# Sixteen partitions of the second K tile go through ScalarE's queue

## The chip, the cores and the metric

The kernel runs on one core of a Trainium2 chip. Five engines work side by side: TensorE (PE in the profile; its weight loads are PEld), VectorE (DVE), ScalarE (ACT), GpSimd (POOL) and SyncE (SP). Sixteen DMA engines move data between HBM and on-chip memory; transfers are issued from SyncE's queue (q1 in the profile) and from ScalarE's (q10). The metric is device time in microseconds, lower is better. The kernel before takes 335.68 us, the median of three runs (335.58 to 337.4).

## What is computed

Attention with grouped heads: 16 batches, 32 query heads over 8 K/V heads, 16 queries per head, 2048 keys, head size 128, all in bf16.

```python
B, Hq, Hkv, Sq, Sk, D = 16, 32, 8, 16, 2048, 128

def reference(q, k, v):
    rep = Hq // Hkv
    k = jnp.repeat(k, rep, axis=1)
    v = jnp.repeat(v, rep, axis=1)
    scores = jnp.einsum("bhqd,bhkd->bhqk", q, k) * D ** -0.5
    p = softmax(scores, axis=-1)
    return jnp.einsum("bhqk,bhkd->bhqd", p, v)
```

K and V are 64 MiB each; everything else is small beside them.

## The kernel before

The 128 pairs of batch and K/V head are taken two at a time, in 64 steps p = 0 to 63 (NP = 64). A step has one K tile and one V tile of 1 MiB, 128 partitions of 8 KB each. Queries come in 16 chunks of four steps, 128 KB each.

For a step, VectorE transposes the K tile (line 474, `KT<-Kn`), PE forms the scores (line 345), VectorE scales them and takes the minimum of the negated scores (line 494), GpSimd joins the two halves (lines 216 to 231), ScalarE takes the exponential (line 542), PE transposes the result (line 363), ScalarE copies that out of PSUM (line 553), and PE multiplies by V (line 415, line 404 in the last steps). The product runs four steps behind the scores (PVLAG = 4). ScalarE then normalises (line 566) and stores (line 573).

K tiles have eight buffers (`Kn`, NK = 8) and V tiles four (`Vb`, NV = 4). SyncE issues nearly all loads in one order written out by hand: the first query chunk (line 166), then for each t the K tile of step t, a query chunk when one is due three steps later, and the V tile of step t - 6 (VLAG = 6). K tile p is issued once the transpose of step p - 8 is done; V tile p once the product of step p - 4 is done; a wait stops everything behind it in SyncE's queue. The first two K tiles are loaded by a plain transfer of 128 rows (line 276), all later ones by the helper `load` (line 171).

Each K buffer has a semaphore, `sem_k`. A transfer adds 16 to the semaphore that it names when all of it has landed. VectorE's transpose of step p waits on it (line 473). After two query chunks are spread out (line 161, by VectorE and GpSimd), PE transposes them (line 378) and ScalarE evicts them (line 528).

ScalarE begins with a table load and a dummy exponential, then issues the second query chunk (in a loop of one round, lines 517 and 518), adds 16 to each of the eight store semaphores, and waits for PE's first query transposes.

Of the kernel before, what the change touches and what calls it, by code (L numbers as in the profile page):

```python
# [11 lines left out]
NK = 8  # L12
# [13 lines left out]
def bass_standalone__gqa_softmax__sampling_kernel(  # L26
# [34 lines left out]
    Kn = [sb(f"Kn{i}", [128, 32 * 128], BF16) for i in range(NK)]  # L61
# [23 lines left out]
    sem_k = [sem(f"sem_k{i}") for i in range(NK)]  # L85
# [26 lines left out]
    kf = k.rearrange("b h s d -> (b h s d)").rearrange("(r x) -> r x", x=4096)  # L112
# [8 lines left out]
    def steps(eng, step, end):  # L121
        for p in range(LO):
            step(p, p)
        with eng.Fori(LO, HI, LOOP) as base:
            for i in range(LOOP):
                step(base + i, LO + i)
        for p in range(HI, end):
            step(p, p)


    def v_tile(p):
        return Kn[p % 4 + (NP - 8) % NK] if p >= NP - 4 else Vb[p % NV]
# [26 lines left out]
    def spread(eng, c, b):  # L159
        src = Qn[c % NQ][:, :, 64 * b:64 * b + 64]  # L160
        return eng.tensor_copy(Q4[:, :, b, :, :], src.unsqueeze(2).to_broadcast([128, 4, 4, 64]))  # L161


    def load_q(eng, c, s):
        src = qf[bass.ds(512 * c, 512), :].rearrange("(a j) d -> a (j d)", j=4)
        eng.dma_start(Qn[s][:, :, :].rearrange("a j d -> a (j d)"), src).then_inc(sem_q[s], 16)  # L166


    def load(eng, dst, src, x, n):
        ap = lambda t, dims: eng.lower_ap_dma(bass.AP(t.tensor, t.offset, dims))  # L170
        return eng.add_instruction(mybir.InstDMACopy(  # L171
            name=nc.get_next_instruction_name(), engine=eng.engine, mode="Copy", queue="qSPDynamicHW",
            ins=ap(src, [[n * x, 128 // n], [1, 1], [1, n * x]]), outs=ap(dst, [dst.ap[0], [1, 1], [1, x]])))
# [3 lines left out]
    with nc.Block() as block:  # L177
# [90 lines left out]
        @block.sync  # L268
        def _(sp):
            def load_k(p):  # L270
                s = p % NK
                if p >= NK:
                    sp.wait_ge(sem_kt, p - NK + 1)
                src = kf[128 * p:128 * (p + 1), :]
                if p < 2:
                    ins = sp.dma_start(Kn[s][:, :], src)  # L276
                else:
                    ins = load(sp, Kn[s][:, :], src, 4096, 2)
                ins.then_inc(sem_k[s], 16)

            def load_v(p):
                if p >= NP - 4:
                    sp.wait_ge(sem_kt, p - 3)
                elif p >= NV:
                    sp.wait_ge(sem_pv, p - NV + 1)
                dst = v_tile(p)[:, :]
                done = sem_vx[p - NP + 4] if NP - 4 <= p < NP - 1 else sem_v[p % NV]
                if p < P4:
                    load(sp, dst, vf[128 * p:128 * (p + 1), :], 4096, 2).then_inc(done, 16)
                    return  # L290
                dst = dst.rearrange("a (g x) -> a g x", g=2)
                src = vf4[:, 2 * p:2 * p + 2, :]
                if p < NP - 1:
                    for h in range(2):
                        load(sp, dst[:, h, :], src[:, h, :], 2048, 2).then_inc(done, 16)
                    return
                for n, x in enumerate((slice(0, 1536), slice(1536, 2048))):
                    sp.dma_start(dst[:, :, x], src[:, :, x]).then_inc(sem_vl[n], 16)

            def store_held(p, n):  # L300
                sp.wait_ge(sem_nm, p + n + 1)
                dst = of[128 * p:128 * (p + n), :].rearrange("(x r) d -> r x d", x=n)
                sp.dma_start(dst, Oh[:, p - PH:p - PH + n, :]).then_inc(sem_oh, 16)

            load_q(sp, 0, 0)
            for t in range(NP + VLAG):
                if t < NP:
                    load_k(t)
                for c in range(2, NQC):
                    if t == 4 * c - QLEAD:  # L310
                        if c == NQ:
                            sp.wait_ge(sem_q4d, 2)
                        sp.wait_ge(sem_q4, max(2, 4 * c - 6))
                        load(sp, Qn[c % NQ][:, :, :], qf[512 * c:512 * (c + 1), :], 512, 2).then_inc(sem_q[c % NQ], 16)
                if 0 <= t - VLAG < NP:
                    load_v(t - VLAG)
            p = PH
            for n in HELD:
                store_held(p, n)
                p += n  # L320
            sp.wait_ge(sem_oh, 16 * len(HELD))
            for s in range(NO):
                sp.wait_ge(sem_o[s], 16 * (PH // NO + 1 + (s == NO - 1)))
# [140 lines left out]
        @block.vector  # L464
        def _(dve):
            def kt(p, i):
                src = Kn[i % NK][:, :].bitcast(F32)
                dst = KT[i % NKT][:, :]
                if isinstance(p, int) and p >= P4:

                    src = src.rearrange("p (m x y) -> p m x y", m=2, x=8)
                    dst = dst.rearrange("p (x m y) -> p m x y", m=2, x=8)
                dve.wait_ge(sem_k[i % NK], 2 * (p - i) + 16 * (i // NK + 1))
                ins = dve.transpose(dst, src)  # L474
                ins.then_inc(sem_kt, 1)

            def recip(p, i, n):
                s = i % NR
                dve.wait_ge(sem_sum[1], p + n)
                dve.reciprocal(rrec[:, s:s + n], rowsum[:, s:s + n]).then_inc(sem_rec, n)  # L480

            def step(p, i):
                known = isinstance(p, int)
                dve.wait_ge(sem_s, p + 1)
                if i >= 2:
                    dve.wait_ge(sem_exp, p - 1)
                for h in range(2):
                    if not known or p < P4:
                        dst = Sneg[i % 2][:, :].rearrange("p (t h g l e) -> p h g t l e", t=8, h=2, g=2, e=2)[:, h]
                        src = S_ps[:, 1024 * h:1024 * (h + 1)].rearrange("p (g t e l) -> p g t l e", g=2, t=8, e=2)  # L490
                    else:
                        dst = Sneg[i % 2][:, :].rearrange("p (h t g l f) -> p h g t l f", h=2, t=4, g=2, f=4)[:, h]
                        src = S_ps[:, 1024 * h:1024 * (h + 1)].rearrange("p (g t f l) -> p g t l f", g=2, t=4, f=4)
                    ins = dve.tensor_scalar(  # L494
                        dst, src,
                        -scale, None, op0=ALU.mult, op1=ALU.min, accum_out=own[:, i % NR, h:h + 1],
                    )
                ins.then_inc(sem_max, 1)
                if i >= 3 and i % 2:
                    recip(p - 3, i - 3, 2)  # L500
                if not known or p + 2 < NP:
                    kt(p + 2, i + 2)

            dve.wait_ge(sem_q[0], 16)
            spread(dve, 0, 1).then_inc(sem_q4d, 2)
            for p in range(2):
                kt(p, p)
            steps(dve, step, NP)
            for p in range(NP - 2, NP):
                recip(p, p, 1)  # L510

        @block.scalar
        def _(act):
# [2 lines left out]

            with act.Fori(1, 2, 1) as c:
                load_q(act, c, 1)

            for s in range(NO):  # L520
                act.nop(nofuse=True).then_inc(sem_o[s], 16)
# [106 lines left out]
```

## Time and profile before

| | before |
|---|---|
| median of three runs | 335.68 us (335.58 to 337.4) |
| the profiled execution: time | 335.8 us |
| the profiled execution: span from first to last instruction | 333.9 us |
| bytes moved, mean rate | 138.61 MB, 415 GB/s |
| busy share PE, VectorE, ScalarE, GpSimd | 84%, 88%, 78%, 45% |
| K loads: count, median from issue to landing | 64, 20.2 us |
| V loads of 1 MiB: the same | 56, 18.3 us |
| chain that ended last: DMA, PE, VectorE | 57%, 17%, 16% |

The span is cut into 40 slices of 8.3 us on the page. The chain that ended last is followed back from the last instruction: at each step to what released it. Its DMA part counts from a transfer's issue to its landing, so time that the transfer waited behind others is in it. A row of the timeline gives the start, the duration, the engine, the line, the operation, output and input, and in brackets how long the engine was idle before and what ended that. A row of the windows gives, for one stretch of the span, the busy time and count of PE, PEld, VectorE, ScalarE and GpSimd, then the granted PE clock, the mean busy share of the DMA engines (it can exceed 1 in a short window, because a packet is booked whole where it begins) and GB/s.

### The profile page before, as it was taken

The numbers are of one execution on the slowest core, as the hardware profiler recorded it, in microseconds if no ns is written. First come the engines' busy times: TensorE is split into PE (matmuls) and PEld (weight loads), VectorE is DVE, ScalarE is ACT, GpSimd is POOL, SyncE is SP. The second block draws the span as 40 slices with busy tenths as digits, with TensorE's granted clock in tenths as the row PEclk, the third lists the DMA queues.
The fourth block names the chain that finished last, engine by engine and source line by source line (L and its number), as shares of the span: only waits on it lengthen the run. The fifth ranks groups of instructions, "written<-read, shape, count | busy, mean of one in ns | idle before, by whom it ended". The sixth has DMA issues, their size and how long they took to land.

```text
span 333.9 us, 16112 instructions
## 1 busy us (share of the span) xinstructions
PE 279.1 (84%) x6542; PEld 209.1 (63%) x6542; DVE 294.8 (88%) x354; ACT 258.8 (78%) x482; POOL 149.4 (45%) x488
## 2 busy tenths in 40 slices
PE   2557979999998989888897988979879798788786
PEld 1234757777776766666665766757657567667464
DVE  3999998999999989989898898998999989999930
ACT  3286887989897979779688787887878787886873
POOL 4444455353645544354445435354363453543330
PEclk9996999999999999999999999999999999999999
DMA  8999999999999999999999999999999999999997
GB/s 316 422 412 432 413 412 426 418 425 422 426 422 431 427 422 425 423 422 425 420 426 421 424 422 426 430 417 428 421 425 422 426 420 418 426 422 413 409 408 261
DMA packets 21854, 138.61 MB, mean 415 GB/s; under 512 B 11472, under 2 KB 11984, under 8 KB 13136
## 3 DMA queue, kind: packets, MB, share of 16 engines
q1 hardware_dynamic: 14640, 136.69, 97.7%
q10 hardware_dynamic: 7200, 1.74, 2.4%
q8 instruction: 8, 0.13, 0.2%
q14 instruction: 6, 0.05, 0.0%
HBM read 136.31 MB, written 2.10 MB: 415 GB/s over the span
## 4 chain that ended last, share of the span: by engine, by line
DMA 57%; PE 17%; DVE 16%; issue 7%; ACT 1%; SPq 1%; POOL 1%; DVEq 0%; POOLq 0%
DMA Vb<-in_v_dram 44%; PE O_ps L415 10%; DVE KT L474 9%; DMA Kn<-in_k_dram 8%; DVE Sneg L494 7%; DMA Kn<-in_v_dram 5%; PE ST_ps L363 3%; PE S_ps L345 3%; ACT P L542 1%; SPq L171 1%; PE ST_ps L378 1%; PE ST_ps L404 0%; POOL nbias L224 0%; SPq L276 0%; SPq L166 0%
## 5 line engine op out<-in xcount | busy, mean ns | idle before, releaser
L474 DVE STREAM_TRANSPOSE KT<-Kn 128x2048 f32<-128x2048 f32 x64 | 147.7, 2308 | 21.0 <-DMA Kn<-in_k_dram 20.9
L542 ACT ACTIVATE P<-Sneg,nbias 128x1024 bf16<-128x1024 f32 x128 | 146.0, 1142 | 15.1 <-POOL nbias L224 13.2
L494 DVE TENSOR_SCALAR_CACHE_REDUCE Sneg<-S_ps 128x1024 f32<-128x1024 f32 x128 | 149.9, 1206 | 3.0 <-PE S_ps L345 2.8
L415 PE MATMUL O_ps<-Vb,PT 64*64 64x128 bf16 x3584 | 111.1, 216 | 30.9 <-issue 26.8
L415 PEld LDWEIGHTS O_ps<-Vb,PT 64*64 64x64 bf16 x3584 | 102.9, 107 | 49.9 <-issue 49.9
L553 ACT ACTIVATE PT<-ST_ps 128x512 f32<-128x512 f32 x126 | 68.5, 594 | 15.7 <-PE ST_ps L363 15.0
L345 PE MATMUL S_ps<-KT,Qs 32*64 32x512 bf16 x2048 | 74.3, 399 | 6.0 <-DVE Sneg L494 3.9
L363 PE MATMUL ST_ps<-ident,P 128*128 128x128 f32 x504 | 69.7, 282 | 8.3 <-ACT P L542 8.3
L216 POOL COPY oth<-own 64x4 f32<-64x4 f32 (+1 forms) x65 | 11.9, 183 | 136.4 <-DVE Sneg L494 134.3
L363 PEld LDWEIGHTS ST_ps<-ident,P 128*128 128x128 f32 x504 | 54.7, 142 | 16.6 <-ACT P L542 10.9
L345 PEld LDWEIGHTS S_ps<-KT,Qs 32*64 32x64 bf16 x2048 | 27.6, 106 | 30.5 <-issue 17.1
L198 POOL COPY Qs<-QT 128x512 bf16<-128x512 bf16 x64 | 39.0, 610 | 12.1 <-POOL rowsum L231 6.0
L224 POOL TENSOR_SCALAR nbias<-own,oth 128x1 f32<-128x1 f32 x128 | 33.9, 280 | 10.6 <-POOL oth L219 9.0
L566 ACT ACTIVATE O<-O_ps,rrec 128x128 bf16<-128x128 f32 x48 | 17.5, 365 | 26.6 <-PE O_ps L415 26.5
L161 POOL COPY Q<-Qn 128x1024 bf16<-128x1024 bf16 x31 | 32.4, 1044 | 1.3 <-DMA Qn<-in_q_dram 1.3
L231 POOL TENSOR_TENSOR rowsum<-own,oth 64x1 f32<-64x1 f32 x128 | 23.8, 186 | 8.2
L378 PEld LDWEIGHTS ST_ps<-ident,Q 128*128 128x128 f32 x128 | 14.4, 148 | 18.3 <-issue 18.3
L378 PE MATMUL ST_ps<-ident,Q 128*128 128x128 f32 x128 | 22.1, 300 | 4.5 <-POOL Q L161 4.5
L542 ACT ACTIVATION_READ_ACCUMULATOR P<-Sneg,nbias 128x1 f32 x128 | 24.1, 188 | 0.0
L528 ACT ACTIVATE QT<-ST_ps 128x512 f32<-128x512 f32 x32 | 18.5, 578 | 3.7 <-PE ST_ps L378 3.7
L219 POOL COPY oth<-own 64x4 f32<-64x4 f32 (+1 forms) x65 | 11.8, 181 | 7.3
L566 ACT ACTIVATE Oh<-O_ps,rrec 128x128 bf16<-128x128 f32 x12 | 4.4, 367 | 9.6 <-PE O_ps L415 6.7
(30 smaller groups left out, 44.6 us busy)
## 6 DMA issues: line engine op xcount, KB each, us to landing
Kn<-in_k_dram SPq DMA_DIRECT2D x64, 1024.0 KB, 20.2
Vb<-in_v_dram SPq DMA_DIRECT2D x56, 1024.0 KB, 18.3
Vb<-in_v_dram SPq DMA_DIRECT2D x8, 512.0 KB, 15.6
Kn<-in_v_dram SPq DMA_DIRECT2D x6, 512.0 KB, 14.7
Qn<-in_q_dram SPq DMA_DIRECT2D x15, 128.0 KB, 20.0
out_dram<-O ACTq DMA_DIRECT2D x49, 32.0 KB, 8.9
Kn<-in_v_dram SPq DMA_DIRECT2D x1, 768.0 KB, 17.7
out_dram<-Oh SPq DMA_DIRECT2D x3, 128.0 KB, 15.8
```

Of the source, the lines that this page charges most:

```text
L161: return eng.tensor_copy(Q4[:, :, b, :, :], src.unsqueeze(2).to_broadcast([128, 4, 4, 64]))
L198: gp.tensor_copy(Qs[i % 2][:, :, :], QT[i // 4 % 2][:, :, 128 * x:128 * (x + 1)].bitcast(BF16)).then_inc(sem_qs, 1)
L224: ins = gp.tensor_scalar(nbias[:, s, h:h + 1], own[:, s, h:h + 1], oth[:, s, h:h + 1], None, op0=ALU.min)
L231: gp.tensor_tensor(rowsum[rows, t:t + 1], own[rows, s, 2 + h:3 + h], oth[rows, s, 2 + h:3 + h], op=ALU.add,).then_inc(sem_sum[h], 1)
L345: ins = pe.matmul(S_ps[64 * w:64 * (w + 1), 512 * r:512 * (r + 1)], qs[rows, b, f, 64 * h:64 * (h + 1)], kt[rows, w, b, f], start=(acc == ...
L363: ins = pe.transpose(dst[:, 128 * t:128 * (t + 1)], P[i % 2][:, 128 * x:128 * (x + 1)], ident4[:, :])
L378: ins = pe.transpose(dst[:, 128 * j:128 * (j + 1)], src[:, j, b, :], ident4[:, :])
L415: ins = pe.matmul(out[rows, :], pt[rows, w, t, e, :], vt[rows, x, :], start=(x == 0), stop=(x == 31),)
L474: ins = dve.transpose(dst, src)
L494: ins = dve.tensor_scalar(dst, src, -scale, None, op0=ALU.mult, op1=ALU.min, accum_out=own[:, i % NR, h:h + 1],)
L542: ins = act.activation(to[:, h], of_s[:, h], ACT.Exp, bias=nbias[:, s, h:h + 1], scale=-1.0, accum_out=own[:, t, 2 + h:3 + h],)
L553: act.activation(PT[i % NPT][:, 4 * h:4 * (h + 1), :].rearrange("p t q -> p (t q)"), p_stage_ap(p, h), ACT.Copy,).then_inc(sem_ev[h], 1)
```

## The change

The load of the second K tile (step 1) is cut in two. SyncE loads partitions 16 to 127 of it, at its place in SyncE's order; ScalarE loads partitions 0 to 15, rows 128 to 143 of K, directly behind its load of the second query chunk. Both add 16 to the same semaphore, `sem_k[1]`, so the transposes that use K buffer 1 (steps 1, 9, 17 and so on) wait for 16 more than before. Nothing else is changed: the same bytes are loaded to the same places.

```diff
                 src = kf[128 * p:128 * (p + 1), :]
-                if p < 2:
+                if p == 1:
+                    ins = sp.dma_start(Kn[s][16:128, :], src[16:128, :])
+                elif p == 0:
                     ins = sp.dma_start(Kn[s][:, :], src)
                 else:
                     ins = load(sp, Kn[s][:, :], src, 4096, 2)
...
-                dve.wait_ge(sem_k[i % NK], 2 * (p - i) + 16 * (i // NK + 1))
+                dve.wait_ge(sem_k[i % NK], 2 * (p - i) + 16 * (i // NK + 1 + (i % NK == 1)))
                 ins = dve.transpose(dst, src)
...
             with act.Fori(1, 2, 1) as c:
                 load_q(act, c, 1)
 
+            act.dma_start(Kn[1][0:16, :], kf[128:144, :]).then_inc(sem_k[1], 16)
+
             for s in range(NO):
                 act.nop(nofuse=True).then_inc(sem_o[s], 16)
```

## The prediction

> **What bounds the kernel now.** I read the page first (parts 2, 3 and 6), then the chain of waits, then the timeline of the first 45 us, then windows of a quarter of a microsecond over the start, because the change touches nothing after it.
>
> The page shows a transfer stream that never pauses.
>
> ```profile
> DMA  8999999999999999999999999999999999999997
> GB/s 316 422 412 432 413 412 426 418 425 422 426 422 431 427 422 425 423 422 425 420 426 421 424 422 426 430 417 428 421 425 422 426 420 418 426 422 413 409 408 261
> ...
> q1 hardware_dynamic: 14640, 136.69, 97.7%
> ```
>
> The first two rows are the 40 slices: the 16 DMA engines are busy in all of them, at 408 to 432 GB/s except in the first and the last. The third says that SyncE's queue alone takes 97.7% of the engines' time. The page's list of issues gives 20.2 us from issue to landing for a K tile and 18.3 us for a V tile, of which moving 1 MiB takes 2.5 us (1.049 MB at 422 GB/s): a load waits some 16 us behind others. So the end of the kernel is the start of the stream, plus all bytes at the stream's rate, plus a tail. The tail, from the chain of waits (start, duration, what):
>
> ```profile
> 312.66 17.69 DMA Kn<-in_v_dram
> 330.39 1.14 PE ST_ps L404 x32
> 331.56 0.37 ACT O L566
> ```
>
> The last V pieces land at 330.35 (312.66 + 17.69), one product and one normalisation follow, then the last store. A change moves the end if it moves the start of the stream, its bytes, its rate, or lets it run dry.
>
> The start, by the timeline (start, duration, engine; "q" is an engine's sequencer issuing; in brackets the idle time and what ended it):
>
> ```profile
> 0.72 0.40 SPq L166 DMA_DIRECT2D Qn<-in_q_dram  x1
> ...
> 0.92 0.39 ACTq L166 DMA_DIRECT2D Qn<-in_q_dram  x1
> ...
> 1.17 0.89 SPq L276 DMA_DIRECT2D Kn<-in_k_dram  x2
> ...
> 5.68 0.60 ACT L528 ACTIVATE QT<-ST_ps 128x512 f32<-128x512 f32 x1 [3.46 <-PE ST_ps L378]
> 6.06 2.31 DVE L474 STREAM_TRANSPOSE KT<-Kn 128x2048 f32<-128x2048 f32 x1 [2.60 <-DMA Kn<-in_k_dram]
> ...
> 8.66 2.31 DVE L474 STREAM_TRANSPOSE KT<-Kn 128x2048 f32<-128x2048 f32 x1 [0.29 <-DMA Kn<-in_k_dram]
> ```
>
> The reader is to see: both K loads are issued by 2.06; the first K is in at 6.06, the second at 8.64 (the chain has its landing there, 7.00 us after 1.64), so 1 MiB takes 2.58 us here; VectorE waits 0.29 us for the second K; ScalarE has nothing to do for 3.46 us before 5.68. The windows at that time (the last two columns are DMA share and GB/s):
>
> ```profile
> 2.50:2.75 0.25, 0.00 (x0) 0.00 (x0) 0.00 (x0) 0.00 (x0) 0.00 (x0) 1.00 2.20 524
> 2.75:3.00 0.25, 0.00 (x0) 0.00 (x0) 0.00 (x0) 0.00 (x0) 0.00 (x0) 1.00 1.42 356
> 3.00:3.25 0.25, 0.00 (x0) 0.00 (x0) 0.22 (x1) 0.00 (x0) 0.19 (x1) 1.00 0.00 0
> 3.25:3.50 0.25, 0.00 (x0) 0.00 (x0) 0.21 (x1) 0.00 (x0) 0.25 (x1) 1.00 1.01 426
> ```
>
> There is a hole as the stream goes over from queries to the first K: no packet begins between 3.00 and 3.25. Packets are booked where they begin, so I take the three windows from 2.50 to 3.25 together: (524 + 356 + 0) / 3 = 293 GB/s against 422, that is 129 x 0.75 = 97 KB short, or 0.23 us of stream.
>
> **The change, part by part.**
>
> *SyncE's second K issue* stays one instruction, of 112 rows of 8 KB instead of 128, at the 0.42 to 0.45 us of line 276. Even if it cost nothing, what follows on SyncE's queue is four K loads from 2.10, for data wanted after 8.6. Zero on the path, either way.
>
> *ScalarE's added issue* is one instruction at the 0.39 us of its row, from 1.31 to 1.70, ahead of eight increments and of the eviction that begins at 5.68 after 3.46 us of idleness. Hidden by that; with the cover gone it would put 0.39 us on the evictions, and these feed scores that wait for the first transposed K until 8.5 anyway.
>
> *The bytes* are the same: 16 rows of 8 KB (131 KB, 0.31 us at 422 GB/s) go over from one queue to the other. From the first issue at 0.72 to the first window with real traffic (1.75 to 2.00, 172 GB/s) is about 1.0 us; so ScalarE's rows can move from about 2.3 to 2.7, beside the first K and just ahead of the hole. What that is worth no row shows: at best the whole hole, -0.23 us; at worst nothing. I take -0.1, nearer to nothing, since the hole is seen with two queues already at work (ScalarE's queries were issued at 0.92).
>
> [...]
>
> *The first K comes later* by up to 0.31 us if ScalarE's rows go in ahead of it: its transpose begins at 6.37 and ends at 8.68. The next transpose waits for the second K until 8.66 today, so it moves by 0.02 us at most. PE's first scores move from 8.52 to 8.83 and end by 10.8, before VectorE is free for them (10.97). Covered; without that cover 0.31 us would pass into the chain of compute.
>
> *The second K's wait* now takes 32 increments instead of 16: both pieces must be in. Behind it in VectorE's queue stand the scaling of the first scores and the third transpose; PE's second scores and SyncE's load of K9 (issued at 11.00) wait for these. As all its bytes are in the stream by the time that they are today, I expect the landing at 8.4 to 8.7.
>
> *How late compute may be* before the stream notices is the cover behind all this. SyncE issues nothing between these two lines:
>
> ```profile
> 17.07 0.59 SPq L171 DMA_DIRECT2D Kn<-in_k_dram  x1
> 36.53 0.47 SPq L171 DMA_DIRECT2D Vb<-in_v_dram  x1
> ```
>
> V4 waits for the first product. By then 11 K, 4 V and 4 query loads are issued: 15 x 1024 + 4 x 128 KB = 16.25 MB, 38.5 us at 422 GB/s, so the stream has work until about 40.3 (begun at 1.75). V4's bytes can move from 37.6 (36.53 plus that 1.0). The slack is some 2.7 us; a later compute chain costs only what exceeds it.
>
> *The pace of the rows.* The trace has no load of 112 or of 16 partitions. Bounds from the nearest rows: at the pace of the first two K loads (2.58 us a MiB) nothing is lost; at half that pace SyncE's 112 rows, 7/8 of 2.58 = 2.26 us, take 2.26 us more, and at a quarter ScalarE's 16 rows, 0.32 us, take 0.97 us more. I take 0: the nearest rows are whole loads of the same row length.
>
> Sum: -0.1 + 0 + 0 = -0.1. The profiled execution has a span of 333.9 and a time of 335.8 (1.9 around it), which becomes 335.7; it lies 0.12 above the median of the runs, 335.68, so by the median 335.6.
>
> **The rivals.**
>
> *The start gains more.* Over 2 to 4 us the stream moved 318 GB/s instead of 422: 104 x 2 = 208 KB, 0.49 us. If a second supply of big rows closed all of it: 335.2. Against: half of that loss lies before 2.5, before any K row can move. [...]
>
> *The rows collide, and it is slower.* Place: the second K, 2.6 to 8.7 us. Today every load covers all 128 partitions; both pieces now cover part of them, and their rows are dealt out anew. If engines get into each other's way, the stream stands behind them, and nothing later makes it up, since it is full to the end. Price: 0.97 + 2.26 = 3.2 us by the bounds above, 338.9; it decides the verdict from 1.68 us on, that is where about half of it comes true. For it: no row shows such a shape run well. Against: it must hold for most of the 112 rows. [...]
>
> *Supply runs dry.* If the compute start came over 2.7 us later, V4 would be late and the stream would idle for the rest; at 5 us later +2.3, 338.0. The granted PE clock is 0.69 from 25 to 30 us and 0.81 from 30 to 40, just ahead of V4, so such delays exist; but the change delays compute by 0.02 us.
>
> **How the numbers follow.** The forecast (-0.25 to +0.4 us about the median) 0.63; the start gains more, within 0.5%, 0.08, beyond it 0.07; collisions 0.17, of which 0.11 beyond 0.5%; supply dry or the like 0.05, all beyond it. So faster 0.07, slower 0.16, same 0.77. The predicted time is the forecast's, 335.6. The range goes from 335.0 (the whole early loss, and the 0.1 by which the runs fall below their median) to 337.4 (the estimate by ports of +1.3, and the highest of the runs shown); beyond it I leave about 0.07 below and 0.12 above.
>
> **What would show it.** The second transpose on VectorE begins between 8.4 and 8.7; the windows at 3.00 to 3.25 hold bytes; the first begins up to 0.3 us later; V4 is issued within 0.3 us of 36.5; the slices stay at 408 to 432 GB/s; the last V lands at 330.1 to 330.5. I am wrong if the second K lands after 9.5, if a dip follows in the windows from 3 to 9, or if the middle of the stream, which the change doesn't touch, runs at another rate.

## The result and the profile after

The changed kernel takes 338.45 us (median of 22 runs, 337.53 to 341.88) against 335.9 us for the kernel before (22 runs, 335.58 to 339.14): 1.0074 times as long, 95% interval 1.0056 to 1.0092. It is slower by 2.5 us, which is under 1% but clear of the noise; the prediction had said 335.6 us, no change, with a range that ended at 337.4. The profiled execution after has a span of 335.7 us and a time of 337.63, 1.8 above those before.

The same rows of the page, of the changed kernel, and under them the row of ScalarE's queue (q10; before, 1.74 MB and 2.4%):

```profile
DMA  8999999999999999999999999999999999999998
GB/s 245 403 414 420 418 412 415 429 429 420 425 422 425 427 419 429 424 423 422 423 424 421 431 424 421 420 425 430 415 432 420 424 420 420 428 418 418 409 409 265
...
q1 hardware_dynamic: 14624, 136.55, 97.6%
q10 hardware_dynamic: 7232, 1.87, 2.5%
```

The DMA engines are booked as busy throughout, as before, yet in the first slice they moved 245 GB/s instead of 316. So the busy share doesn't tell here how fast the bytes move. From the second slice on the rates are those of before. Stage by stage, in the windows of the kernel before (last column GB/s):

```profile
5.00:12.00 7.00, 3.37 (x39) 1.70 (x37) 5.65 (x3) 1.19 (x2) 2.15 (x3) 1.00 1.04 438
12.00:38.00 26.00, 18.62 (x300) 11.69 (x308) 25.54 (x32) 19.02 (x34) 12.67 (x41) 0.87 1.01 418
38.00:70.00 32.00, 29.55 (x732) 22.61 (x716) 30.81 (x39) 27.35 (x52) 14.85 (x49) 1.00 1.01 420
70.00:300.00 230.00, 200.81 (x4914) 153.27 (x4912) 212.98 (x254) 187.09 (x349) 108.67 (x352) 1.00 1.01 423
```

and of the changed one:

```profile
5.00:12.00 7.00, 3.25 (x40) 1.78 (x38) 3.67 (x2) 1.20 (x2) 2.15 (x3) 1.00 1.04 322
12.00:38.00 26.00, 18.56 (x265) 11.42 (x258) 24.65 (x28) 16.18 (x29) 10.85 (x36) 0.93 1.01 420
38.00:70.00 32.00, 28.04 (x678) 21.36 (x680) 29.87 (x39) 26.86 (x52) 14.50 (x48) 1.00 1.01 418
70.00:300.00 230.00, 202.86 (x4974) 155.29 (x4959) 214.72 (x259) 188.29 (x352) 110.05 (x353) 1.00 1.01 424
```

All of the loss lies in the seven microseconds from 5 to 12: (438 - 322) x 7 / 422 = 1.9 us of stream. Afterwards the two run alike, so the stream stays 1.9 us behind to its end. The start of the changed kernel in its timeline:

```profile
1.50 0.35 ACTq L522 DMA_DIRECT2D Kn<-in_k_dram  x1
1.64 0.42 SPq L276 DMA_DIRECT2D Kn<-in_k_dram  x1
...
7.81 2.31 DVE L476 STREAM_TRANSPOSE KT<-Kn 128x2048 f32<-128x2048 f32 x1 [4.28 <-DMA Kn<-in_k_dram]
...
10.64 2.31 DVE L476 STREAM_TRANSPOSE KT<-Kn 128x2048 f32<-128x2048 f32 x1 [0.52 <-DMA Kn<-in_k_dram]
```

Both issues are made when they were meant to be made. But the first K is in at 7.81 instead of 6.06, and the second at 10.6 instead of 8.64. V4 follows, and at the end the last piece of V:

```profile
38.53 0.47 SPq L171 DMA_DIRECT2D Vb<-in_v_dram  x1
```

```profile
332.21 0.92 PEld L406 LDWEIGHTS ST_ps<-Kn,PT 128*64 128x64 bf16 x32 [0.42 <-DMA Kn<-in_v_dram]
```

V4 is issued 2.0 us later than before, and the last product waits for V until 332.2 instead of 330.4: the 1.8 us by which the span grew.

### The profile page after: what moved, and what is told of

The parts are those of the page before. It is cut to its first block, busy times and chain, and to the rows that moved or that the text cites. A ratio compares the mean times of both kernels' runs of the same rounds, so it can differ in the third digit from the quotient of the medians.

```text
span 335.7 us, 16119 instructions
## 1 busy us (share of the span) xinstructions
PE 281.0 (84%) x6542; PEld 210.2 (63%) x6542; DVE 294.5 (88%) x354; ACT 258.5 (77%) x482; POOL 150.2 (45%) x488
## 4 chain that ended last, share of the span: by engine, by line
DMA 52%; DVE 17%; PE 16%; issue 9%; ACT 3%; POOL 1%; SPq 1%; DVEq 0%; POOLq 0%; ACTq 0%
DMA Vb<-in_v_dram 43%; DVE KT L476 9%; DVE Sneg L496 8%; DMA Kn<-in_k_dram 8%; PE O_ps L417 7%; PE ST_ps L365 3%; ACT P L546 3%; PE S_ps L347 2%; PE O_ps L406 1%; POOL nbias L224 1%; PE ST_ps L427 1%; PE S_ps L406 1%; PE ST_ps L406 1%; PE ST_ps L380 0%; PE S_ps L365 0%
## 5 line engine op out<-in xcount | busy, mean ns | idle before, releaser
L365 PE MATMUL ST_ps<-ident,P 128*128 128x128 f32 x504 | 71.2, 286 | 7.8 <-ACT P L546 7.8
L365 PEld LDWEIGHTS ST_ps<-ident,P 128*128 128x128 f32 x504 | 56.0, 145 | 16.3 <-ACT P L546 9.8
L224 POOL TENSOR_SCALAR nbias<-own,oth 128x1 f32<-128x1 f32 x128 | 34.2, 283 | 10.6 <-POOL oth L219 9.0
```

The lines of the kernel that those rows point to most:

```text
L224: ins = gp.tensor_scalar(nbias[:, s, h:h + 1], own[:, s, h:h + 1], oth[:, s, h:h + 1], None, op0=ALU.min)
L365: ins = pe.transpose(dst[:, 128 * t:128 * (t + 1)], P[i % 2][:, 128 * x:128 * (x + 1)], ident4[:, :])
```

## The experiments

Theory R: the pieces of the second K cover only part of the 128 partitions, and such rows are written slowly, which holds up the whole stream. Its sharper form P, for the 16 rows: they are slow because they go to neighbouring partitions. Theory Q: two queues at once disturb the stream. Theory S: a late start of compute leaves the stream dry later on. Ratios are to the kernel before on the same chip.

The edits shown leave out unchanged lines (`...`). With one queue, with the cut by columns and with the cut at partition 64 they are edits of the changed kernel; all others are edits of the kernel before. Where a spare tile is loaded, the lines that allocate it and that wait for its load at the end of the kernel are left out too. The windows come from one profiled execution of each kernel, which need not be the median one; where it isn't, the text says so.

### One queue for both pieces

```diff
-                    ins = sp.dma_start(Kn[s][16:128, :], src[16:128, :])
+                    sp.dma_start(Kn[s][16:128, :], src[16:128, :]).then_inc(sem_k[s], 16)
+                    ins = sp.dma_start(Kn[s][0:16, :], src[0:16, :])
...
-            act.dma_start(Kn[1][0:16, :], kf[128:144, :]).then_inc(sem_k[1], 16)
```

> The second K in the same two pieces (112 rows, then 16), both issued by SyncE; ScalarE loads only its queries. Theory R (rows: pieces that cover only part of the partitions are written slowly): the stream loses the same 1.5 to 2 us between 5 and 10 us, time +1.5 to +2.5 us over the kernel before, while the first K lands at about 6.1 as before, because nothing runs ahead of it. Theory Q (two queues at once disturb the stream): like the kernel before, within 0.3 us.

Measured: 337.94 us against 335.8, 1.0061 (1.0044 to 1.0077), +2.1. The first transpose begins at 6.50, and the window from 5 to 12 us is:

```profile
5.00:12.00 7.00, 3.36 (x39) 1.69 (x37) 3.23 (x2) 1.19 (x2) 2.15 (x3) 1.00 1.05 314
```

The second queue isn't needed for the loss: R's forecast holds, and Q falls as the whole cause. What ScalarE's queue adds in the changed kernel is a later first K (7.81).

### The second K cut by columns

```diff
-                    ins = sp.dma_start(Kn[s][16:128, :], src[16:128, :])
+                    ins = sp.dma_start(Kn[s][:, 512:4096], src[:, 512:4096])
...
-            act.dma_start(Kn[1][0:16, :], kf[128:144, :]).then_inc(sem_k[1], 16)
+            act.dma_start(Kn[1][:, 0:512], kf[128:256, 0:512]).then_inc(sem_k[1], 16)
```

> The second K is cut by columns, not by partitions: SyncE loads 7 KB of each of 128 rows, ScalarE 1 KB of each of 128 rows; the same 1/8 of the bytes goes through ScalarE's queue at the same place. Theory R: within 0.4 us of the kernel before, no slow stretch between 5 and 10 us. Theory Q: +1.5 to +2.5 us as in the changed kernel.

Measured: 336.77 us (335.86 to 337.92), 1.0030 (1.0019 to 1.0042), +1.0. From 5 to 12 us 399 GB/s, a loss of (438 - 399) x 7 / 422 = 0.6 us: a third of the changed kernel's. The second K is complete only at 10.5 and the stream runs at 406 instead of 420 GB/s from 38 to 70 us, which is theory S, below. This profile is of the slowest of the ten executions (337.92, +2.1), and the fastest, 335.86, was no slower than the kernel before, so the two losses hold for that execution. Why the columns cost 0.6 us at the start stays open; R expected under 0.4.

### ScalarE loads the whole second K

```diff
-                if p < 2:
+                if p == 1:
+                    return
+                if p == 0:
                     ins = sp.dma_start(Kn[s][:, :], src)
...
+            act.dma_start(Kn[1][:, :], kf[128:256, :]).then_inc(sem_k[1], 16)
```

> ScalarE loads the whole second K in one piece of 128 rows, SyncE none of it. Theory R: within 0.4 us of the kernel before, though the first K may land later (its rows share the engines with the second K's). Theory Q: at least the loss of the changed kernel, +1.8 us or more, since eight times as many rows run beside SyncE's.

Measured: 341.0 us, 1.0164 (1.0147 to 1.0181), +5.2; no theory had that right in full. From 5 to 12 us the stream runs at 440 GB/s (438 before), so eight times as many rows beside SyncE's cost it nothing, and Q falls a second time. The loss is elsewhere, in the windows of this run:

```profile
38.00:40.00 2.00, 2.00 (x64) 1.65 (x50) 1.81 (x4) 2.00 (x3) 1.77 (x3) 1.00 1.01 418
40.00:42.00 2.00, 2.00 (x52) 1.65 (x54) 2.00 (x4) 1.75 (x6) 0.70 (x5) 1.00 0.44 172
42.00:44.00 2.00, 2.00 (x58) 1.25 (x44) 2.00 (x2) 1.88 (x4) 1.14 (x4) 1.00 0.90 303
```

The DMA share falls to 0.44: here the engines really have nothing to do. ScalarE's load of the second K took 11.5 us from issue to landing, among SyncE's third and later K tiles; the second transpose began at 13.03 instead of 8.66, and V4 was issued at 40.79 instead of 36.53. This made theory S. The profile is of the fastest of five executions (339.52, +3.7); what the others lose beyond that is not known.

### Sixteen rows more, next to each other and apart

The second K stays whole; ScalarE loads 16 of its rows once more into a spare tile, in the first run into partitions 0 to 15, in the second into 0, 7, ... 105. The second edit is shown against the first.

```diff
+            act.dma_start(spare[0:16, :], kf[128:144, :]).then_inc(sem_sp, 16)
```

> SyncE loads the whole second K as before; ScalarE additionally loads 16 rows into a spare tile, at the place where the changed kernel does. Added bytes alone are 0.31 us. Theory R with the 16 rows as a culprit (quarter pace): +0.9 to +1.3 us. Theory R with the 112 rows as the culprit: +0.3 us. Theory Q: +1.5 to +2.5 us.

```diff
-            act.dma_start(spare[0:16, :], kf[128:144, :]).then_inc(sem_sp, 16)
+            act.dma_start(spare[0:106:7, :], kf[128:144, :]).then_inc(sem_sp, 16)
```

> As the run with 16 additional rows on ScalarE's queue, but they go to partitions 0, 7, 14, ... 105 of the spare tile instead of 0 to 15; the same bytes, rows and queue. [...] Theory F (few long rows on a second queue cost, wherever they go): +1.2 us again.

Measured: +1.17 us with neighbours (336.97 against 335.8, 1.0037, 1.0023 to 1.0051), +0.42 us with rows apart (336.32 against 335.9, 1.0015, 1.0005 to 1.0025). Windows of the run with neighbours:

```profile
5.00:6.00 1.00, 1.00 (x7) 1.00 (x6) 0.00 (x0) 0.25 (x1) 0.00 (x0) 1.00 1.22 360
6.00:7.00 1.00, 0.51 (x3) 0.10 (x1) 0.00 (x0) 0.75 (x2) 0.00 (x0) 1.00 1.01 188
7.00:8.00 1.00, 0.00 (x0) 0.00 (x0) 0.29 (x1) 0.20 (x1) 0.74 (x2) 1.00 0.86 336
```

and with rows apart:

```profile
5.00:6.00 1.00, 1.00 (x6) 1.00 (x6) 0.00 (x0) 0.27 (x1) 0.00 (x0) 1.00 0.97 393
6.00:7.00 1.00, 0.48 (x3) 0.08 (x1) 0.41 (x1) 0.75 (x2) 0.00 (x0) 1.00 1.07 360
7.00:8.00 1.00, 0.00 (x0) 0.00 (x0) 1.00 (x1) 0.18 (x1) 0.76 (x2) 1.00 0.98 401
```

Same bytes, same rows, same queue and place; only the partitions that they are written to differ, and 188 GB/s between 6 and 7 us becomes 360. P holds and F falls: without the 0.31 us of bytes the neighbours cost 0.86 us, the others 0.11. That the placement of the rows decides is shown; why it does is not.

### The 112 rows by themselves

SyncE loads rows 16 to 127 of the second K once more, into a spare tile, behind the second K; and as a control all 128. By theory R the 112 rows are slow; its rival puts all of the loss on the 16.

```diff
+                if p == 1:
+                    sp.dma_start(spare[16:128, :], src[16:128, :]).then_inc(sem_sp, 16)
```

> The kernel before, and SyncE additionally loads rows 16 to 127 of the second K into partitions 16 to 127 of a spare tile, behind the second K. Bytes alone: 7/8 of 2.48 us = +2.2 us. [...] Rival (112 rows are as good as 128, all the loss comes from the 16): +2.0 to +2.4 us.

> Control: the same with all 128 rows of the second K loaded once more into the spare tile. Both theories: the bytes alone, 1 MiB at 422 GB/s, +2.3 to +2.7 us, no slow stretch.

Measured against 335.9: the 112 rows +3.57 us (339.47, 1.0103, 1.0086 to 1.0120), all 128 rows +2.52 us (338.42, 1.0074, 1.0057 to 1.0091). An eighth fewer bytes take 1.05 us longer, so the rival falls. Windows of the run with 112 rows more:

```profile
8.00:9.00 1.00, 0.08 (x8) 0.11 (x16) 0.77 (x1) 0.00 (x0) 1.00 (x2) 1.00 1.01 336
9.00:10.00 1.00, 1.00 (x24) 0.55 (x32) 0.49 (x1) 0.00 (x0) 0.39 (x1) 1.00 1.09 328
10.00:11.00 1.00, 0.85 (x16) 0.00 (x0) 1.00 (x1) 0.00 (x0) 0.00 (x0) 1.00 1.21 344
11.00:12.00 1.00, 0.00 (x0) 0.00 (x0) 1.00 (x2) 0.00 (x0) 0.00 (x0) 1.00 0.91 295
```

Four windows at 295 to 344 GB/s, booked as full. The control has 410 to 467 there; its second and third:

```profile
9.00:10.00 1.00, 1.00 (x24) 0.58 (x32) 1.00 (x1) 0.00 (x0) 0.37 (x1) 1.00 0.97 410
10.00:11.00 1.00, 0.90 (x23) 0.02 (x7) 1.00 (x1) 0.00 (x0) 0.00 (x0) 1.00 1.10 467
```

Beyond their bytes (2.2 us) the 112 rows cost 1.4 us. With the 16 rows' 0.86 that makes some 2.3, near the 1.9 us that the changed kernel's stream loses; the two pieces were measured one at a time, as additional loads.

### A late start alone

```diff
+            dve.wait_ge(sem_k[1], 16)
             for p in range(2):
                 kt(p, p)
```

> The kernel before, but VectorE's first transpose waits for the second K too, so that compute begins some 2.6 us later while the loads stay as they are. Theory S (a late start of compute leaves the stream dry at about 40 to 60 us once it exceeds a slack of about 1.1 us, read from the run where ScalarE loads the whole second K): the second transpose begins at about 11.0 instead of 8.7 (+2.3), V4 is issued at about 38.8, and the time rises by 1.0 to 1.6 us. The prediction's slack of 2.7 us: no loss, within 0.3 us.

Measured: 339.19 us (336.85 to 340.02), 1.0091 (1.0065 to 1.0116), +3.3 in the median, +2.3 in the profiled execution (338.24). The loads are those of before. In the timeline the transposes now stand together:

```profile
8.78 4.51 DVE L474 STREAM_TRANSPOSE KT<-Kn 128x2048 f32<-128x2048 f32 x2 [5.24 <-DMA Kn<-in_k_dram]
```

V4 is issued at 39.73, 3.2 us later than before, and the windows from 38 to 70 us show 389 GB/s instead of 420, a loss of (420 - 389) x 32 / 422 = 2.4 us. So 0.8 us of the delay was covered. Only 0.7 us of the loss falls before 44 us (389, 291 and 410 GB/s in the windows of 2 us from 38, against 414, 404 and 418 before). The rest is spread from there to 70: V6 is issued at 50.20 instead of 45.94, so the later V loads are late as well. With the whole second K on ScalarE: 4.26 us of delay, (420 - 373) x 32 / 422 = 3.6 us lost, 0.7 covered. Theory S holds: a late start alone leaves the stream short. The expectation's 1.0 to 1.6 us was too small, because the delay had grown from 2.4 us at the second transpose to 3.2 at V4.

### Four pieces in the middle of the stream

```diff
+                if t in (20, 25, 30, 35):
+                    if t > 20:
+                        sp.wait_ge(sem_sp, 16 * ((t - 20) // 5))
+                    sp.dma_start(spare[0:16, :], kf[128:144, :]).then_inc(sem_sp, 16)
```

> The kernel before, and SyncE additionally loads 16 rows into partitions 0 to 15 of a spare tile at four places in the middle of the stream (with the K tiles of steps 20, 25, 30 and 35): 4 x 0.31 = 1.25 us of bytes. [...] Rival (only the start is sensitive): +1.0 to +1.6 us.

Measured: 343.68 us against 335.85, 1.0224 (1.0167 to 1.0282), +7.8: not the start alone, and more than four times the 1.17 us that one such piece cost there (4.7). Windows where the pieces pass:

```profile
90.00:95.00 5.00, 5.00 (x140) 3.68 (x124) 5.00 (x7) 4.62 (x9) 3.08 (x10) 1.00 1.03 311
...
120.00:125.00 5.00, 3.35 (x87) 2.40 (x81) 3.42 (x6) 3.78 (x8) 2.83 (x8) 1.00 0.94 319
145.00:150.00 5.00, 3.63 (x104) 2.96 (x96) 3.37 (x5) 3.40 (x8) 2.79 (x9) 1.00 1.07 337
```

The first takes (427 - 311) x 5 / 422 = 1.4 us in its window, the next two 1.2 and 1.1, beyond their own bytes; before, these windows moved 427, 423 and 426 GB/s. From 70 to 300 us the stream runs at 413 instead of 423 GB/s, a loss of (423 - 413) x 230 / 422 = 5.5 us, and the pieces' bytes are 1.2 us: together 6.7 of the 7.1 us of the profiled execution (342.93). So the loss is that of the stream, here too. Why a piece costs more than 0.86 us here isn't settled.

### The cut at partition 64

```diff
-                    ins = sp.dma_start(Kn[s][16:128, :], src[16:128, :])
+                    ins = sp.dma_start(Kn[s][64:128, :], src[64:128, :])
...
-            act.dma_start(Kn[1][0:16, :], kf[128:144, :]).then_inc(sem_k[1], 16)
+            act.dma_start(Kn[1][0:64, :], kf[128:192, :]).then_inc(sem_k[1], 16)
```

> The changed kernel with the cut at partition 64: ScalarE loads partitions 0 to 63, SyncE 64 to 127 of the second K. [...]

Measured: 337.75 us, 1.0052 (1.0028 to 1.0076), +1.9; 311 GB/s from 5 to 12 us, (438 - 311) x 7 / 422 = 2.1 us. Two pieces of 64 partitions lose as much as those of 16 and 112 (1.9 us), as theory R has it. V4 is issued at 39.73, 3.2 us late, yet the stream runs at 420 GB/s from 38 to 70.

### Queries on ScalarE's queue

```diff
-            load_q(sp, 0, 0)
...
+            load_q(act, 0, 0)
             with act.Fori(1, 2, 1) as c:
                 load_q(act, c, 1)
```

> A version that might beat the kernel before: both first query chunks are issued by ScalarE, so SyncE's first issue is the first K and the stream starts with long rows; the second K stays whole on SyncE. The hole at 3 us and the slow ramp are worth at most 0.5 us. The queries land later (about 4.6 instead of 3.0), but the first scores wait for the first transpose until 8.4 anyway. Expected -0.3 to 0 us; if the queries come after 6 us the late start costs +0.5 us or more.

Measured: 338.8 us, 1.0071 (1.0046 to 1.0096), +3.0. The first queries are spread at 6.35 instead of 3.03; why they come that late was not tested. V4 came at 39.69, and the stream ran at 395 instead of 420 GB/s from 38 to 70 us, 1.9 us short, as in the late start. In the other windows from 5 to 300 us it ran as before (438, 418 and 424 GB/s), so the rest of the 3 us lies before 5 or after 300 us; what it is, is open. No version that beats the kernel before was found.

### The changed kernel once more

> The changed kernel once more, beside the others of this chip. Loss of the stream by the pieces alone: +1.8 to +2.1 us, as in the profiled execution. Theory S (a part of the executions loses more, because V4 is issued later than the slack allows): median +2.3 to +2.9 us and single executions above +3; without S, +1.8 to +2.1 throughout.

Measured: 338.02 us (337.60 to 338.65) against 335.85 (335.67 to 340.14), +2.2; the ratio, 1.0034 (0.9998 to 1.007), is loose because this chip's runs of the kernel before scatter upward too. 321 GB/s from 5 to 12 us, 418 from 38 to 70: in the profiled execution (337.78, +1.9) again the start alone. Neither expectation was met in full: seven of the ten executions lie above +2.1, none above +3. What the slower ones lose is not in this profile. In two of them, at 338.10, the span is 335.6 and 335.7 us, no longer than in the fastest (335.7), so there the difference lies outside the instructions. The first 22 runs lay 2.5 us apart in their medians and 1.95 in their lowest; what makes up the 0.6 us between is open.

## Why the prediction was wrong, point by point

- *What bounds the kernel* was right: a full stream to the end, in which nothing lost at the start is made up. The 1.9 us lost by 12 us are in the span at the end (1.8).
- *The pace of the rows* is the step that failed. It took 0 because "the nearest rows are whole loads of the same row length". The nearest rows differed in what mattered: they cover all 128 partitions. Measured beyond their bytes: 0.86 us for the 16 rows (bound 0.97) and 1.4 us for the 112 (bound 2.26). The bounds had it between them; their quarter and half pace were the author's assumption, which no run had shown. And the rival "the rows collide, and it is slower", with 1.68 us (0.5% of 335.68) as the point of decision, is what happened; it had 0.11 beyond that point. Each piece is shown to be slow by a run of its own; what in the hardware its rows wait for is not.
- *The range* ended at 337.4, though the prediction's own bounds of the unshown shape reached 338.9; the measured 338.45 lies between. No run shows the +1.3 us "by ports" that goes into its upper end; in its place the runs showed 0.86 us for the 16 rows and 1.4 for the 112, each by itself, and 1.9 us lost by the changed kernel's stream.
- *The hole at 3 us*, taken at -0.1, was worth 0: over the first 5 us the stream moved 231 GB/s, against 229 before. The window from 3.00 to 3.25 of the changed kernel moved 33 GB/s. ScalarE's rows weren't there in time, as its transfers show (columns: KB, us from issue to landing):

```profile
Kn<-in_k_dram SPq DMA_DIRECT2D x1, 896.0 KB, 9.0
...
Kn<-in_k_dram ACTq DMA_DIRECT2D x1, 128.0 KB, 6.5
```

  131 KB issued at 1.50 took 6.5 us; the packet records have their first row at 4.8, when 93 of SyncE's rows of 8 KB had begun. By the issue of the queries I had expected them from 2.3 to 2.7.
- *The first K* was said to be late by at most 0.31 us; it was late by 1.75, as it shared the stream with slow rows: it was as late with the 16 neighbouring rows more (its transpose began at 7.71), and less with the rows apart (6.59). *The wait for 32 increments* was said to end at 8.4 to 8.7; it ended at 10.6. Both are more than the covers named there. Yet neither cost time by itself, by the next point.
- *The slack of compute* was put at 2.7 us and is about 1: the late start and the whole second K on ScalarE covered 0.8 and 0.7, the queries on ScalarE 1.3, and with one queue V4 came 3.2 us late, 1.1 more than the stream's own 2.1, without a loss from 38 to 70. The sum had counted V4's bytes alone; in the late start most of the loss came with the V loads after it. The slack saved the changed kernel all the same: V4 came 2.0 us later, but the stream was 1.9 us behind too. "Supply runs dry" was the wrong rival here, but it is cheap to trigger: a late start costs this kernel 2.4 us and more.
- *Both issues* cost nothing, as said: 0.42 and 0.35 us, hidden.
- One reading beside the sum was off: of the 208 KB missing from 2 to 4 us, about a third lies before 2.5 (197 and 385 GB/s in the two windows), not half.
- *The tail* of the kernel before is slow while its DMA engines are booked as busy: from 329 to 332 us their mean share is 1.10, 0.98 and 0.91, and the stream moves 343, 251 and 195 GB/s. The cause is open.

## What to carry to other kernels

In this stream, which is full to the end, a load paid for the pace of its rows, not only for its bytes: the same 131 KB cost 1.2 us in 16 neighbouring partitions and 0.4 in 16 apart, and 112 partitions cost more than 128 (3.57 us against 2.52). Here it was best to leave the second K on all 128 partitions in one piece and on SyncE's queue: 335.9 us, where the versions that cut it or moved it took 336.8 to 341.0. Where a shape doesn't occur in the trace, let its bounds, not its nearest look-alike, set the range. A first tile that landed later was free here only up to the slack of the buffers that wait for compute, about 1 us, and a run that delays the start on purpose measures that slack.

## What was not expected of the hardware

The DMA engines were booked at a share of about 1 while moving 188 GB/s (1.01 from 6 to 7 us with 16 neighbouring rows more) and while moving 423 (1.01 from 70 to 300 us before), so here the share didn't tell the slow stream from the fast one; GB/s did. ScalarE's 16 rows, issued 1.5 us after the start, first moved at 4.8. And the stretch in which TensorE's clock was granted at about half speed lay elsewhere in each profile: at 0.50 from 28 to 32 us before, at 0.54 from 30 to 32 us after, at 0.50 from 32 to 36 us with the whole second K on ScalarE.
